# Windowed attention and routed experts in one kernel: from step 13 on, transposes of xa open the next step and the gate logits move behind the scores

## The chip, the cores and the metric

One core of a Trainium2 chip runs the whole program. The metric is the device time of one execution in microseconds (us). The program is compiled once; its instructions stand in a fixed order on each of the five engines (PE for matrix products and transposes, DVE and ACT for vector and scalar work, POOL, and SP, which issues most transfers), and engines wait for one another by semaphores. DMA engines move data between the device's memory and the on-chip buffers.

## The reference

Attention over a causal window of 64 positions, 8 batches x 8 heads x 576 positions x 64 columns, is followed by a layer of 8 experts in which each row goes to one expert. Which rows an expert gets depends on the data.

```python
def _attn_ref(q, k, v):                      # (8, 8, 576, 64)
    scores = scale * np.matmul(q, k.transpose(0, 1, 3, 2))
    mask = (rel >= 0) & (rel < 64)           # rel = row - column
    attn = softmax(np.where(mask, scores, -1e9))
    return np.matmul(attn, v)

def _moe_ref(x, modality_id, w_gate, modality_bias, w1, w2):   # x: (4608, 512)
    logits = x @ w_gate + modality_bias[modality_id]           # 8 experts
    e_idx = np.argmax(logits, axis=1)
    gate_w = softmax(logits)[rows, e_idx]
    for e in range(8):
        mask = e_idx == e
        out[mask] = gate_w[mask, None] * (np.maximum(x[mask] @ w1[e], 0) @ w2[e])
```

## The kernel before, in words

The 4,608 rows are 36 pairs of blocks (128 rows each). The outer loop is a software pipeline of steps `s` = 0 to 39; step `s` holds work on several pairs at once. From step 13 on (`s > FIRST`, `FIRST` is 12) one step runs, in the order of the code:

- `values(s-2)`: PE multiplies the softmax of pair s-2 by v into the PSUM tile `av`. `logits(s-3)`: PE multiplies `xaT` (the attention output of pair s-3, transposed) by the gate weights, DVE adds the bias (`lg`, L749). `values_out(s-2)`: DVE scales `av` into `xa` (`rw` L723, `xa` L726).
- `scores(s)`: PE, into the two PSUM tiles `sp0` and `sp1` (L659). `minima(s)`: DVE, eight masked row minima, four from each `sp` (L673). `probs_t(s-1)`: PE transposes the softmax of the pair before in two groups of four (`ss`), ACT copies each out (`pT`).
- `exps(s)`: ACT, in three portions. Between them stand four places (`gap`) that each take the next piece of expert work from the generator `slot_pieces`.
- Behind the second gap: `ranks()` in odd steps (PE counts the rows of each expert over a group of two pairs, DVE reads them into `tgt` and `cnt`), `x_t(s-2)` (PE transposes `xa` of pair s-2, ACT copies to `xaT`, L736), then `part(0)`. Behind the third gap: `part(1)`. A part prepares half the heads of q or k for a later group of two pairs: either PE transposes them ("plain" heads, tile `qk`) and DVE or ACT copies them out, or DVE transposes them itself (L585). How many heads are plain depends on the group (`n_plain`: all 8, 4 or none).

Expert work comes in slots of 256 rows, 16 pieces, so four steps. A piece `first` (L321) is 12 products of 256 columns into a quarter of the hidden layer in the PSUM tile `em`; two such pieces fill `em`, then ACT writes `hh` (L329) and DVE `hl` (L330) from it. A piece `second` (L343) is 6 products of 512 columns into `y0` or `y1`. In steps 13, 14, 15, 17, 18, 19, ... the four gaps hold first, first, second, second. In every fourth step (16, 20, ..., 36) they hold second, first, first, second, because there one slot ends and the next begins: DVE turns the next slot's rows (`xt` L283) and splits them (`xl` L196), ACT writes `xh` (L195). Until the loop ends, every `first` uses the one tile `em` (it has one buffer).

Two PSUM tiles `tp0` and `tp1` are used in turn (`turn_bank`) for what PE transposes, for the ranks and, before the change, for the logits. A tile is written again only when its last reader is done. Rows of `xa` lie in five buffers; each is scattered to memory by POOL (L828) and may be overwritten by a later `values_out` only when that transfer has landed. Work on the routing tables waits in lists (`routing`, `held`), from which `tick` and `release` put instructions on DVE.

After step 39 (from about 344 us) the program holds expert work alone.

Of the kernel before, what the change touches and what calls it, by code (L numbers as in the profile page):

```python
# [19 lines left out]
P = 128  # L20
# [6 lines left out]
def tile_window_attn_moe(  # L27
# [24 lines left out]
    GB = 2  # L52
# [476 lines left out]
    def turn_bank(s):  # L529

        i = n_tp[0]
        n_tp[0] += 1
        if s < FIRST and i % 5 > 1:
            return ps_m.tile([P, 512], F32, name=("em", "y0", "y1")[i % 5 - 2])
        return tp_bank()
# [125 lines left out]
                    rhs=kT[rows, win(c, hp), :], start=True, stop=True)  # L661
        st[p, "sp"] = sp

    def minima(p):

        sp = st.pop((p, "sp"))
        mask = masks[:, 1 if 2 * p % BPB == 0 else 2 if (2 * p + 1) % BPB == 0 else 0]
        ss = [work.tile([P, HP, P], F32, name="ss", bufs=3) for _ in range(2)]
        mn = small.tile([P, H], F32, name="mn")
        for u in range(H):  # L670
            a, hp = divmod(u, HP)
            h = 2 * hp + a
            nc.vector.tensor_tensor_reduce(  # L673
                out=ss[a][:, hp, :], in0=sp[a][:, hp * P:(hp + 1) * P], in1=mask,
                scale=-1.0 / 8.0, scalar=3.0e38, op0=ALU.add, op1=ALU.min,
                accum_out=mn[:, h:h + 1])
        sm = small.tile([P, H], F32, name="sm")
        st[p, "s"] = ss, mn, sm

    def exps(p, us):  # L680
        ss, mn, sm = st[p, "s"]
# [56 lines left out]
    def logits(p, lt):  # L738
        G, j = divmod(p, GB)
        xaT = st.pop((p, "xT"))  # L740
        for c in range(NC1):
            for i in range(2):
                cols = slice(c * P + i * W64, c * P + (i + 1) * W64)
                nc.tensor.matmul(  # L744
                    out=lt[i * W64:(i + 1) * W64, 0:E], lhsT=xaT[:, cols], rhs=wg[:, c, :],
                    start=(c == 0), stop=(c == NC1 - 1))
        if j == 0:
            st[G, "lg"] = small.tile(sh3, F32, name="lg")
        nc.vector.tensor_tensor(  # L749
            out=st[G, "lg"][:, j, :], in0=lt[:, 0:E], in1=bias_sel[:, p, :], op=ALU.add)  # L750
# [5 lines left out]
    def release():  # L756

        if held:
            tick(len(routing))
            held.pop(0)()  # L760
# [319 lines left out]
    for s in range(NPR + 4):  # L1080
        j = s % GB
        if s <= FIRST:
            for f, args in at.pop(s, ()):
                f(*args)
        n_tick = 6 if s < FIRST else 5
        n_gap = 0 if s < FIRST else 4
        G = s // GB + 1
        heads = PARTS[j] if G < NG else ()
        R = (s - 5) // GB if s >= 5 and j == 1 else -1

        def loads(n):

            for f, args in at.get(s, [])[:n]:
                f(*args)
            at[s] = at.get(s, [])[n:]

        def part(i):
            if not heads:
                return
            if 2 * 2 * i >= n_plain(G, heads[i][0]):  # L1100
                turn_heads(G, *heads[i])
                return
            tp = turn_bank(s)
            heads_t(G, *heads[i], tp)
            heads_out(tp, G, *heads[i], nc.scalar.copy if heads[i] == K1 else nc.vector.tensor_copy)

        def ranks():
            if R < 0:
                return None
            tp = turn_bank(s)  # L1110
            rk = route2(R, tp)
            n = None
            if R == NG - 1 or any(R == T for T, _ in EARLY):
                n = counts_out(tab if R == NG - 1 else pl, counts(R, tp))
            route3(R, rk)
            return n
        if 1 <= s < FIRST:
            swap_upper(s - 1)

        if 2 <= s < NPR + 2:  # L1120
            values(s - 2)
            if s <= FIRST:
                values_out(s - 2)
        if 3 <= s < NPR + 3:
            logits(s - 3, turn_bank(s) if s != FIRST else ps_m.tile([P, 512], F32, name="y0"))
            if (s - 3) % GB == GB - 1:
                route1((s - 3) // GB)
        if FIRST < s < NPR + 2:
            values_out(s - 2)
        if s < NPR:  # L1130
            scores(s)
            if s == FIRST:
                x_turn(fetched[0])
                gap(it, True)
            minima(s)
            if s == FIRST - 2:
                tick(todo[0][-1] - issued[0], table=True)
        if 1 <= s <= NPR:
            if s == FIRST:
                run_later()  # L1140
            if s >= FIRST:
                swap_upper(s - 1)
            swap_v(s - 1)
            for a in range(2):
                probs_t(s - 1, a, turn_bank(s))
            sums(s - 1)
        if s < NPR:
            exps(s, (0, 1))
        if s == 0:
            first_pair(1, (both[:1], both[1:]))  # L1150
            cast_bias()
        if s <= FIRST:
            if s >= 2:
                x_t(s - 2, turn_bank(s) if s != FIRST else ps_m.tile([P, 512], F32, name="y0"))
            run_later()
            tick(2)
            if s < NPR:
                exps(s, (2, 3, 4))
            part(0)
            if s == FIRST:  # L1160
                weights(s)
                gap(it, True)
            run_later()
            tick(n_tick)
            cnt = ranks()
            exps(s, (5, 6, 7))
        else:
            gap(it, True)
            run_later()
            release()  # L1170
            tick(2)
            if s < NPR:
                exps(s, (2, 3, 4))
            if s < FIRST + 4 or s % 2:
                weights(s)
            loads(3)
            gap(it, True)
            cnt = ranks()
            if s < NPR + 2:
                x_t(s - 2, turn_bank(s))  # L1180
            part(0)
            run_later()
            tick(n_tick)
            loads(1)
            if s < NPR:
                exps(s, (5, 6, 7))
        if n_gap > 2:
            if FIRST <= s < FIRST + 4:
                weights(s)
            gap(it, True)  # L1190
        part(1)
        run_later()
        tick(n_tick)
        if s > FIRST:
            loads(1)
        if s == WEIGHTS:
            load_weights()
        if s >= WEIGHTS:
            weights(s)
        if s > FIRST:  # L1200
            loads(9)
        if n_gap > 3:
            gap(it, True)
        run_later()
        if s == 1:
            select_bias()
        if s == 4:
            nc.sync.dma_start(out=xs_blk[DUMMY:DUMMY + 2].rearrange("b p c -> p b c"), in_=padrow)
        for T, xs_ in EARLY:
            if T == R:  # L1210
                plan(T, xs_, cnt)
# [292 lines left out]
```

## Time and profile before

| | us |
|---|---|
| median of 3 runs | 612.1 (611.96 to 615.05) |
| profiled execution | 611.99, granted clock 0.995 |
| span of its profile | 610.2 |
| PE busy in the span | 590.4 (97%) |
| DVE, ACT, POOL busy | 377.2, 283.0, 152.6 |

The profile is one execution. Its span runs from the first to the last instruction of the program; the execution's time is 1.8 us more. PE's busy time includes the modelled ends of products that overlap, so it does not say how much time could be saved; the distances between the starts of instructions do. In the rows below, "<-" in brackets names what ended the idle time before an instruction, and a tile's name stands without its buffer number.

### The profile page before, as it was taken

The page shows a single profiled execution, that of the slowest core. Times are in us where ns is not written, and L with a number is a line of the kernel's source. Part 1 is how long each engine was busy: PE and PEld are TensorE (multiplying, and loading weights), DVE is VectorE, ACT ScalarE, POOL GpSimd, SP SyncE. Part 2 cuts the span into 40 slices and gives each one's busy share as a digit, 9 for nine tenths or more (in the row PEclk, how much of TensorE's full clock was granted, in tenths as well). Part 3 has the DMA queues.
Part 4 walks back from the last instruction along what each step waited for, and adds up shares of the span by engine and source line. Part 5 has one row for each costly group of instructions (what it writes and reads, how often), then busy time and mean ns, then how long its engine had stood idle before and what let it go on. Part 6 is the DMA issues. An engine that isn't in the chain of part 4 may idle for free.

```text
span 610.2 us, 17296 instructions
## 1 busy us (share of the span) xinstructions
PE 590.4 (97%) x6257; PEld 524.7 (86%) x6257; DVE 377.2 (62%) x1479; ACT 283.0 (46%) x907; POOL 152.6 (25%) x337
## 2 busy tenths in 40 slices
PE   7998889999999999999999999999999999999996
PEld 4887778889898888988888899999999999999983
DVE  4898988877777877678755465323224634765311
ACT  3999986665657565646462111111113522653110
POOL 6323332152232331532423131011001111102102
PEclk9999999999999999999999999999999999999999
DMA  9989877685866755554513034632143544588300
GB/s 169 199 209 249 209 209 172 152 200 138 203 166 160 190 110 144 145 130 84 138 53 106 35 104 133 194 92 69 44 166 90 156 170 118 192 245 255 119 15 37
DMA packets 176615, 87.95 MB, mean 144 GB/s; under 512 B 140378, under 2 KB 158864, under 8 KB 176400
## 3 DMA queue, kind: packets, MB, share of 16 engines
q1 hardware_dynamic: 167184, 66.54, 44.8%
q0 software_dynamic: 6608, 19.71, 8.9%
q8 instruction: 50, 0.82, 0.6%
q10 hardware_dynamic: 2736, 0.58, 0.5%
q14 instruction: 37, 0.30, 0.2%
HBM read 67.36 MB, written 23.78 MB: 149 GB/s over the span
## 4 chain that ended last, share of the span: by engine, by line
PE 76%; DVE 4%; ACT 2%; issue 2%; DMA 2%; SPq 0%; POOL 0%; POOLq 0%; DVEq 0%; ACTq 0%
PE y L343 30%; PE em L321 21%; PE sp L321 10%; PE tp L483 6%; PE av L715 3%; PE sp L659 3%; PE tp L744 1%; ACT ss L685 1%; DMA qk<-in_k_dram 1%; DMA xs_scratch<-xa,idx 1%; DVE ss L673 1%; DVE xl L196 1%; DVE xt L283 1%; PE tp L393 1%; PE em L368 1%
## 5 line engine op out<-in xcount | busy, mean ns | idle before, releaser
L343 PE MATMUL y<-Whi,hh 128*128 128x512 f32 x288 | 115.8, 402 | 0.0
L685 ACT ACTIVATE ss<-ss,mn 128x128 f32<-128x128 f32 x288 | 112.2, 397 | 4.9 <-DMA y<-in_moe_modality_id_dram 2.9
L343 PE MATMUL y<-Wlo,hh 128*128 128x512 f32 x288 | 112.8, 392 | 0.0
L343 PE MATMUL y<-Whi,hl 128*128 128x512 f32 x288 | 112.4, 390 | 0.0
L354 POOL DMA_INDIRECT out_dram<-y,id x36 | 38.8, 1077 | 220.1 <-DVE y L351 156.7
L330 DVE SCALAR_TENSOR_TENSOR hl<-em,hh 128x512 fp32r<-128x512 f32 x50 | 34.5, 691 | 88.2 <-ACT hh L329 78.9
L321 PE MATMUL em<-xh,Whi 128*128 128x256 f32 x400 | 81.6, 285 | 0.3 <-issue 0.3
L321 PE MATMUL em<-xh,Wlo 128*128 128x256 f32 x400 | 79.1, 279 | 0.0
L321 PE MATMUL em<-xl,Whi 128*128 128x256 f32 x400 | 79.1, 279 | 0.0
L329 ACT ACTIVATE hh<-em 128x512 fp32r<-128x512 f32 x50 | 29.9, 598 | 105.0 <-PE em L321 88.5
L694 ACT COPY pT<-tp 128x512 f32<-128x512 f32 x57 | 31.3, 589 | 75.0 <-PE tp L483 71.4
L673 DVE CUSTOM_DVE_ANT_0 ss<-sp,masks 128x128 f32<-128x128 f32 x288 | 63.4, 285 | 2.7 <-PE sp L659 2.0
L321 PEld LDWEIGHTS em<-xh,Whi 128*128 128x128 f32 x400 | 62.8, 188 | 2.6 <-issue 0.2
L343 PEld LDWEIGHTS y<-Whi,hl 128*128 128x128 f32 x288 | 54.1, 188 | 12.1
L343 PEld LDWEIGHTS y<-Whi,hh 128*128 128x128 f32 x288 | 54.2, 188 | 9.5 <-issue 0.8
L343 PEld LDWEIGHTS y<-Wlo,hh 128*128 128x128 f32 x288 | 54.2, 188 | 8.3
L321 PEld LDWEIGHTS em<-xh,Wlo 128*128 128x128 f32 x400 | 60.9, 188 | 0.0
L321 PEld LDWEIGHTS em<-xl,Whi 128*128 128x128 f32 x400 | 60.9, 188 | 0.0
L828 POOL DMA_INDIRECT xs_scratch<-xa,idx x36 | 36.7, 1019 | 88.9 <-issue 48.9
L685 ACT ACTIVATION_READ_ACCUMULATOR ss<-ss,mn 128x1 f32 x288 | 55.9, 194 | 0.0
L329 ACT ACTIVATE hh<-sp 128x512 fp32r<-128x512 f32 x22 | 13.1, 597 | 80.5 <-PE sp L321 74.5
L715 PEld LDWEIGHTS av<-ve,pT 128*64 128x64 f32 x576 | 36.3, 138 | 12.6 <-issue 7.8
(241 smaller groups left out, 1152.9 us busy)
## 6 DMA issues: line engine op xcount, KB each, us to landing
xt<-xs_scratch SPq DMA_DIRECT2D x72, 128.0 KB
vo<-in_v_dram SPq DMA_DIRECT2D x32, 256.0 KB
y<-in_moe_w_dram SPq DMA_DIRECT2D x32, 256.0 KB
vo<-in_moe_w_dram SPq DMA_DIRECT2D x18, 256.0 KB
ss<-in_moe_w_dram SPq DMA_DIRECT2D x18, 256.0 KB
xs_scratch<-xs_scratch SPq DMA_DIRECT2D x8, 514.0 KB
pT<-in_moe_w_dram SPq DMA_DIRECT2D x12, 256.0 KB
qk<-in_k_dram SPq DMA_DIRECT2D x76, 32.0 KB
```

Source lines behind the costliest of these rows:

```text
L321: nc.tensor.matmul(out=hb[:, i * TP:(i + 1) * TP], lhsT=w[buf][:, c0:c0 + P], rhs=x[:, c * TP:(c + 1) * TP], start=(n == 0), stop=(n == le ...
L329: nc.scalar.activation(out=hh, in_=hb, func=AF.Relu),
L330: nc.vector.scalar_tensor_tensor(out=hl, in0=hb, scalar=0.0, in1=hh.bitcast(F32), op0=ALU.max, op1=ALU.subtract)))
L343: nc.tensor.matmul(out=sl["y", t], lhsT=h[:, i * TP + t * P:i * TP + (t + 1) * P], rhs=w[buf][:, c0:c0 + DM], start=(k == 0 and n == 0), s ...
L354: ins = nc.gpsimd.indirect_dma_start(out=out, out_offset=bass.IndirectOffsetOnAxis(ap=sl["id"][:, t:t + 1], axis=0), in_=y, in_offset=None ...
L483: nc.tensor.transpose(out=out_, in_=in_, identity=ident[p0:p0 + n, p0:p0 + n])
L659: nc.tensor.matmul(out=sp[a][c * W64:(c + 1) * W64, hp * P:(hp + 1) * P], lhsT=qT[rows, place(g + c, hp), :], rhs=kT[rows, win(c, hp), :], ...
L673: nc.vector.tensor_tensor_reduce(out=ss[a][:, hp, :], in0=sp[a][:, hp * P:(hp + 1) * P], in1=mask, scale=-1.0 / 8.0, scalar=3.0e38, op0=AL ...
L685: nc.scalar.activation(out=ss[a][:, hp, :], in_=ss[a][:, hp, :], func=AF.Exp, bias=mn[:, h:h + 1], scale=-1.0, accum_out=sm[:, h:h + 1])
L694: nc.scalar.copy(out=pT, in_=pp)
L715: nc.tensor.matmul(out=by_block(av)[c * W64:(c + 1) * W64, a, :, hp, :], lhsT=pT[:, i:i + W64], rhs=(vo if c else ve)[p][:, 2 * hp + a, :] ...
L828: ins = nc.gpsimd.indirect_dma_start(out=xs, out_offset=bass.IndirectOffsetOnAxis(ap=idx[:, j:j + 1], axis=0), in_=xg[j], in_offset=None)
```

## The change

Nothing is added to the computation or taken from it; from step 13 on, work changes places.

- `x_t` of pair s-3 opens step s (from step 14), where it stood as `x_t(s-2)` behind the second gap. `xaT` is thus made and used in the same step.
- `ranks()` follows `values` directly, ahead of `values_out`.
- `logits(s-3)` stands behind `scores(s)` and writes the tile `em` in place of a `tp` tile. Its DVE reader `lg` stands between the fourth and the fifth of the eight minima.
- Parts that PE transposes are both done behind the second gap; parts that DVE transposes keep their places. Both parts are plain in steps 13, 20, 21, 24, 25, 28 and 29.
- `release` is called only if something was held before this step's `ranks()`.

```diff
-    def minima(p):
+    def minima(p, us):
...
-        for u in range(H):
+        for u in us:
...
+        def part_if(i, by_pe):
+            if heads and by_pe == (4 * i < n_plain(G, heads[i][0])):
+                part(i)
...
+        def gates():
+            if 3 <= s < NPR + 3:
+                logits(s - 3, turn_bank(s) if s < FIRST else ps_m.tile([P, 512], F32, name="em" if s > FIRST else "y0"))
+                if (s - 3) % GB == GB - 1:
+                    route1((s - 3) // GB)
+        if FIRST + 1 < s < NPR + 3:
+            x_t(s - 3, turn_bank(s))
         if 2 <= s < NPR + 2:
             values(s - 2)
             if s <= FIRST:
                 values_out(s - 2)
-        if 3 <= s < NPR + 3:
-            logits(s - 3, turn_bank(s) if s != FIRST else ps_m.tile([P, 512], F32, name="y0"))
-            if (s - 3) % GB == GB - 1:
-                route1((s - 3) // GB)
+        if s <= FIRST:
+            gates()
+        else:
+            ripe = len(held)
+            cnt = ranks()
         if FIRST < s < NPR + 2:
             values_out(s - 2)
...
-            minima(s)
+            minima(s, range(H if s <= FIRST else HP))
+        if s > FIRST:
+            gates()
+        if s < NPR:
+            if s > FIRST:
+                minima(s, range(HP, H))
...
-            release()
+            if ripe:
+                release()
...
-            cnt = ranks()
-            if s < NPR + 2:
-                x_t(s - 2, turn_bank(s))
-            part(0)
+            part_if(0, False)
+            part_if(0, True)
+            part_if(1, True)
...
-        part(1)
+        if s > FIRST:
+            part_if(1, False)
+        else:
+            part(1)
```

On PE in step 18 of the program before, the end of `values` (`av`), the logits into a `tp` tile, and the first `scores`:

```order
L715 MATMUL av<-ve,pT 64x2x32
L715 MATMUL av<-vo,pT 64x2x32
L744 MATMUL tp_2955<-wg,xaT 64x8 x8
L659 MATMUL sp_2973<-kT,qT 64x128
L659 MATMUL sp_2974<-kT,qT 64x128
```

On PE in the same step of the changed program, the end of the scores, the logits, the two groups of softmax transposes (`ss`), and the first piece of expert work:

```order
L659 MATMUL sp_2958<-kT,qT 64x128
L659 MATMUL sp_2959<-kT,qT 64x128
L744 MATMUL em<-wg,xaT 64x8 x8
L483 MATMUL tp_3006<-ident_r,ss 128x128 x4
L483 MATMUL tp_3013<-ident_r,ss 128x128 x4
L321 MATMUL em<-xh,Whi_65 128x256 x2
```

The logits have moved behind the scores, and they and the expert piece write the same tile `em`, with eight transposes between them.

On DVE in step 18 of the program before, the bias addition `lg`, the scaling of `av`, and the first of the minima (each is two instructions, into `ss` and `mn`):

```order
L749 TENSOR_TENSOR lg<-tp_2955,bias_sel 128x8
L723 RECIPROCAL rw<-rs 128x16
L726 TENSOR_TENSOR xa_102<-av,rw 128x512
L673 ISA ss,mn<-sp_2973,masks 128x128
L673 ISA mn 128x1
```

On DVE in the same step of the changed program, from the last minimum of `sp0` to the first of `sp1`:

```order
L675 ISA ss,mn<-sp_2958,masks 128x128
L675 ISA mn 128x1
L749 TENSOR_TENSOR lg<-em,bias_sel 128x8
L675 ISA ss,mn<-sp_2959,masks 128x128
L675 ISA mn 128x1
```

`lg` has moved from the head of the step's DVE work to a place behind `rw`, `xa` and four minima.

On PE at the start of step 38, the last one with logits and one without values, scores or softmax transposes, in the program before:

```order
L343 MATMUL y_6559<-Wlo_67,hh 128x512
L343 MATMUL y_6559<-Whi_2520,hl 128x512
L744 MATMUL tp_6566<-wg,xaT 64x8 x8
L321 MATMUL em<-xh,Whi_2520 128x256 x2
L321 MATMUL em<-xh,Wlo_67 128x256 x2
```

The same place in the changed program:

```order
L343 MATMUL y_6552<-Wlo_67,hh 128x512
L343 MATMUL y_6552<-Whi_2513,hl 128x512
L483 MATMUL tp_6559<-ident_r,xa_101 128x128 x4
L744 MATMUL em<-wg,xaT 64x8 x8
L321 MATMUL em<-xh,Whi_2513 128x256 x2
L321 MATMUL em<-xh,Wlo_67 128x256 x2
```

The transposes of `xa`, which stood behind the second gap of step 37, now stand directly ahead of the logits that need them, and those directly ahead of the expert piece that uses the same tile.

## Rows read from the trace of the kernel before

**Rows 1.** The page, busy time of each engine, its share and instructions.

```profile
PE 590.4 (97%) x6257; PEld 524.7 (86%) x6257; DVE 377.2 (62%) x1479; ACT 283.0 (46%) x907; POOL 152.6 (25%) x337
```

**Rows 2.** Stretch, length, busy PE, PEld, DVE, ACT, POOL; clock, DMA share, GB/s.

```profile
84.01:343.63 259.62, 256.97 (x3317) 229.15 (x3317) 191.93 (x858) 149.56 (x527) 83.17 (x163) 1.00 0.57 141
343.63:610.20 266.57, 260.53 (x1689) 233.29 (x1687) 115.47 (x243) 64.76 (x117) 35.39 (x75) 0.99 0.41 126
```

**Rows 3.** PE's waits from 84 to 344 us: in all, times, longest.

```profile
PE tp L483 <- DVE lg L749: 1.6, 4, 0.5
PE tp L483 <- ACT xaT L736: 0.4, 2, 0.2
```

**Rows 4.** Timeline of PE, step 18 (start, length, line, tiles, count).

```profile
136.86 0.27 PE L715 MATMUL av<-ve,pT 128*64 128x64 f32 x1
...
137.85 0.59 PE L744 MATMUL tp<-wg,xaT 128*64 128x8 f32 x16
138.37 1.10 PE L659 MATMUL sp<-kT,qT 64*64 64x128 f32 x32
139.40 1.09 PE L483 MATMUL tp<-ident_r,ss 128*128 128x128 f32 x8
140.25 0.48 PE L321 MATMUL em<-xh,Whi 128*128 128x256 f32 x2
...
143.13 0.60 PE L483 MATMUL tp<-ident_r,xa 128*128 128x128 f32 x4
143.48 0.47 PE L343 MATMUL y<-Whi,hh 128*128 128x512 f32 x1
```

**Rows 5.** Timeline of PE, middle of step 29.

```profile
256.75 0.64 PE L483 MATMUL tp<-ident_r,xa 128*128 128x128 f32 x4
257.37 0.65 PE L483 MATMUL tp<-ident_r,qk 128*128 128x128 f32 x4
```

**Rows 6.** Timeline of DVE, step 18: the first and the fifth minimum.

```profile
139.52 0.29 DVE L673 CUSTOM_DVE_ANT_0 ss<-sp,masks 128x128 f32<-128x128 f32 x1
...
140.37 0.28 DVE L673 CUSTOM_DVE_ANT_0 ss<-sp,masks 128x128 f32<-128x128 f32 x1
```

**Rows 7.** Timeline of DVE, step 13.

```profile
86.86 0.69 DVE L330 SCALAR_TENSOR_TENSOR hl<-em,hh 128x512 fp32r<-128x512 f32 x1 [0.82 <-ACT hh L329]
87.47 0.15 DVE L749 TENSOR_TENSOR lg<-tp,bias_sel 128x8 f32<-128x8 f32 x1
```

**Rows 8.** Timelines of DVE and PE, start of step 21.

```profile
168.01 0.69 DVE L330 SCALAR_TENSOR_TENSOR hl<-em,hh 128x512 fp32r<-128x512 f32 x1 [2.54 <-ACT hh L329]
...
169.88 0.15 DVE L749 TENSOR_TENSOR lg<-tp,bias_sel 128x8 f32<-128x8 f32 x1
...
170.84 0.28 DVE L673 CUSTOM_DVE_ANT_0 ss<-sp,masks 128x128 f32<-128x128 f32 x1
...
171.24 0.36 PE L321 MATMUL em<-xh,Whi 128*128 128x256 f32 x1
```

**Rows 9.** Timelines of DVE and PE, step 33.

```profile
295.19 0.69 DVE L726 TENSOR_TENSOR xa<-av,rw 128x512 f32<-128x512 f32 x1 [2.24 <-DMA xs_scratch<-xa,idx]
...
294.40 0.48 PE L321 MATMUL em<-xh,Whi 128*128 128x256 f32 x2
```

**Rows 10.** Timelines of ACT, PE and DVE, steps 36 to 38.

```profile
319.94 0.27 PE L715 MATMUL av<-ve,pT 128*64 128x64 f32 x1
...
320.43 1.14 ACT L195 CAST xh<-xt 128x512 fp32r<-128x512 f32 x2 [0.82 <-DVE xt L283]
...
334.05 0.64 PE L483 MATMUL tp<-ident_r,xa 128*128 128x128 f32 x4
...
334.78 0.59 ACT L736 COPY xaT<-tp 128x512 f32<-128x512 f32 x1 [6.34 <-PE tp L483]
...
337.38 0.64 PE L744 MATMUL tp<-wg,xaT 128*64 128x8 f32 x16
...
338.07 0.17 DVE L749 TENSOR_TENSOR lg<-tp,bias_sel 128x8 f32<-128x8 f32 x1 [0.94 <-PE tp L744]
```

More of the change, by code (lines that the diff above doesn't have):

```diff
@@ L662, in scores @@
         st[p, "sp"] = sp
-    def minima(p):
-        sp = st.pop((p, "sp"))
+    def minima(p, us):
+        sp = st[p, "sp"]
         mask = masks[:, 1 if 2 * p % BPB == 0 else 2 if (2 * p + 1) % BPB == 0 else 0]
-        ss = [work.tile([P, HP, P], F32, name="ss", bufs=3) for _ in range(2)]
-        mn = small.tile([P, H], F32, name="mn")
-        for u in range(H):
+        if us[0] == 0:
+            st[p, "s"] = ([work.tile([P, HP, P], F32, name="ss", bufs=3) for _ in range(2)],
+                          small.tile([P, H], F32, name="mn"), small.tile([P, H], F32, name="sm"))
+        ss, mn, _ = st[p, "s"]
+        for u in us:
             a, hp = divmod(u, HP)
@@ L676, in minima @@
                 accum_out=mn[:, h:h + 1])
-        sm = small.tile([P, H], F32, name="sm")
-        st[p, "s"] = ss, mn, sm
     def exps(p, us):
```

## The prediction

> **What bounds the kernel now.** The page's busy times come first: PE 97% of the span, DVE 62%, ACT 46% [rows 1]. The table by stretch then splits the span. Steps 13 to 38, which the change touches, take 259.6 us; the expert work behind them takes 266.6 us with PE at a granted clock of 0.99 [rows 2] and holds no instruction that moves, so what PE loses or gains in the first stretch reaches the end of the program undiminished. In that stretch the waits of PE that the profile names are small: 1.6 us in four waits of softmax transposes for `lg`, 0.4 us in two waits for `xaT` [rows 3]. PE is therefore the bound, and the other engines matter only where PE must wait for them. The timeline of an undisturbed step gives PE's own lengths, from start to start: `values` 0.99 (136.86 to 137.85), logits 0.52, scores 1.03, eight softmax transposes 0.85, two `first` pieces 2.88, `x_t` 0.35 [rows 4].
>
> **Waits that go.** Softmax transposes wait for `lg` because `lg` read the `tp` tile that the second group of transposes needs. With the logits in `em` that reason is gone. The idle time is 1.6 us; from start to start the four places are each about 0.15 us longer than that, since an end is modelled 0.2 us or so behind the next possible start, which makes 2.2 us (an estimate). The plain part behind the third gap waited for ACT's copy of `xaT`, 0.4 us idle in two places and by the same correction 0.7 us; with both plain parts side by side, their `tp` tiles were last read by the `pT` copies, microseconds before. One of each pair of effects is bounded by the idle time alone: 2.0 us in all is the low end, 3.1 us the value I take (it includes about 0.2 us for shorter delays that the wait view does not list).
>
> **PE's own work.** No instruction goes, but neighbours change. `x_t` cost 0.35 us in the middle of step 18 [rows 4] and 0.62 us in step 29, where a plain part followed it [rows 5]. At the front of a step, between `second` and `values`, no row shows it; four transposes at the pitch of the softmax group (0.85 for eight) are 0.43, and 0.35 is the lowest row. Where no part follows, `first` now meets `second` directly; where two plain parts stood apart, `second` is cut once less. Bounds per step: nothing gained (0.35 against 0.35) and 0.27 us gained (0.62 against 0.35). I take 0.15 us for 24 steps, 3.6 us; the ends are 0 and 6.5.
>
> **Waits that come.** `em` has one buffer. In each step a `first` piece now waits until DVE has done `lg`, and `lg` stands behind `rw`, `xa` and four minima. Undisturbed, PE comes to that piece 0.40 + 0.99 + 1.03 + 0.52 + 0.85 = 3.8 us after the step's start (odd steps a little more, for the ranks). DVE starts its minima 0.12 us after the scores are issued (139.40 to 139.52), needs 0.85 for four (139.52 to 140.37) [rows 6] and 0.17 for `lg` [rows 10]: 0.40 + 0.99 + 1.03 + 0.12 + 0.85 + 0.17 = 3.56. So the edit is hidden by 0.2 us of softmax transposes, no more. If DVE is late by more than that, PE waits for the rest. Behind DVE's own waits everything else on DVE queues, `lg` with it. The cases:
>
> - *Step 13.* It starts at 84.01 [rows 2]. `hl` ends at 87.55 because ACT's `hh` was late [rows 7]. `hl` reads `em`, so the logits themselves cannot start before that; then `lg` follows `rw`, `xa` and four minima. From the start of an old `lg` to the first minimum are 0.96 us (169.88 to 170.84) [rows 8], so the new `lg` ends at 87.47 + 0.96 + 0.85 + 0.17 = 89.45. PE by itself would come to `first` at 84.01 + 0.99 + 1.03 + 0.52 + 0.85 = 87.4 (this step has no `x_t` in front). Wait 2.0; the 0.5 that softmax transposes waited here is in the sum above.
> - *Steps 17, 21, 25* follow a slot's end. In step 21 `hl` starts at 168.01, released by ACT, and by the same chain the new `lg` ends at 169.88 + 0.96 + 0.85 + 0.17 = 171.86 [rows 8]. ACT reaches `hh` about 0.55 us sooner, as its `xaT` copy (0.59 [rows 10], less overlap) no longer stands ahead of it: 171.3. PE came to `first` at 171.24 [rows 8]; two waits of step 20 go, about 0.8, and the step's own `x_t`, 0.4, comes in front: 170.8. Wait 0.5; I take it for the three steps, 1.5. If ACT brings nothing it is 1.1 each and as much in step 29, 4.4; if DVE starts such a step early, 0. I am nearer the low end, as the copy does leave ACT's queue by the order.
> - *Step 33.* `xa` waits until 295.19 for the landing of the scatter that empties its buffer; PE had started `first` at 294.40, untouched by it [rows 9]. Now `lg` comes 0.69 + 0.85 + 0.17 behind the start of `xa`: 296.9. Wait 2.5. The Trainium skill (PSUM — Partial Sum Buffer, section "Engine vs sequencer instructions") says that the queues of VectorE and ScalarE are strictly first in, first out. By that rule the wait of `xa` is paid by `lg` in full, as in the sum; could `lg` pass `xa`, this item would be 0 and the sum 2.5 us less. Two more steps have a shorter wait of this kind in front of `xa`; I add 0.3.
> - *Step 36.* Without scores. It starts at 319.94; ACT's `xh` runs until 321.57 [rows 10], so the copy of `xaT` ends near 322.15, and the logits wait from 319.94 + 0.40 + 0.99 = 321.3: 0.8. *Step 37.* No scores either, and `lg` stands behind the ranks' reader, `rw` and `xa`, some 0.17 + 0.24 + 0.69, and takes 0.17, while PE has only the logits, 0.52, to do: 0.75, with the signals between engines 0.9 (an estimate). *Step 38.* `x_t`, ACT's copy and the logits follow one another with nothing between. The copy starts 0.73 us after `x_t` (334.05 to 334.78) and takes 0.59; `lg` starts 0.69 after the logits (337.38 to 338.07) and takes 0.17 [rows 10]: with the signals `first` starts 2.3 us into the step, where PE alone needs 0.40 + 0.52. 1.4.
>
> New waits: 2.0 + 1.5 + 2.5 + 0.3 + 0.8 + 0.9 + 1.4 = 9.4 us.
>
> **Edits costed at nothing.** `ranks` ahead of `values_out`: PE reaches them right behind `values`, and DVE reads them in time in which it stood waiting for the logits. No transfer changes its place on SP or POOL; the scatters are released at the same step and gap as before, since what `ranks` holds back is released one step later in both versions. `xaT` in the same step has 1.03 us of scores and 0.99 of `values` as cover for 0.73 + 0.59, save in steps 36 and 38.
>
> **Sum.** 9.4 - 3.1 - 3.6 = +2.7 us on the profiled execution's 612.0, which is 0.1 below the median: 614.7 us, 0.4% slower.
>
> **The rivals.**
>
> 1. *Forecast* (0.50): waits at `em` cost a little more than the freed waits and the shorter PE work give back; 611.5 to 617.
> 2. *DVE falls behind at every slot boundary* (0.30, slower by over 0.5%). The place is the same chain hh, hl, `lg` in steps 17, 21, 25, 29. It decides if the `first` of step 21 starts more than 0.6 us behind its transposes. With 4.4 in place of 1.5: 617.6. For it: the 2.54 us that DVE stood waiting for ACT in step 21 [rows 8]; against it: the copy that leaves ACT.
> 3. *PE's shorter work and the freed waits win* (0.15, faster). If the scatter of step 33 lands before DVE needs it, and DVE is on time in 17 to 31, only 13 and 36 to 38 are left, 5.1 us; against 3.1 + 5.0 (a gain of 0.2 a step, between the middle and the upper row) the time is 609.0, and with the upper 0.27 a step 607.5. For it: PE waited for DVE four times only in this stretch [rows 3]. Against it: `lg` had no minima ahead of it then.
> 4. *The change moves only cover* (0.05): `em`'s waits appear, but the pieces behind them run closer and the sum is within 0.5 us of before, 612.
>
> **From cases to numbers.** 0.5% of 612.1 is 3.1 us, about what a measurement of this kernel tells from no change. Faster than 609.0: case 3, 0.15. Slower than 615.2: case 2 and the upper part of case 1, 0.30 + 0.10 = 0.40. The rest 0.45. The range from 609.0 to 618.5 leaves out about 0.1 on either side: its low end is case 3, its high end case 2 and 0.9 us for step 33 landing still later. The forecast alone would span 611.5 to 617.
>
> **What would show it.** Right: no wait of softmax transposes for `lg` and none of plain parts for `xaT`; instead waits of PE at L321 `em` for `lg`, largest in steps 13, 33 and 37; a wait of the logits for `xaT` in steps 36 and 38; steps 14, 18 and 22 shorter by about 0.1 us. Wrong would be: PE's waits for `lg` at `em` under 4 us in all (then 3), or over 10 (then 2); `xa` no longer waiting for its scatter in step 33; steps that lengthen without a wait, which would mean that `x_t` at the front costs more than in the middle.

## The result, and the profile after

620.1 us (median of 4, 618.3 to 620.4) against 612.0 for the kernel before on the same chip: ratio 1.0120, 95% interval 1.0085 to 1.0154. A second measurement of the same kernel (below) gave 1.0091, 1.0066 to 1.0115. Slower by about 1%, in the direction of the forecast; the first value lies above its range (609.0 to 618.5), the second in it. Kernels below are compared with the kernel before as it ran beside them on their chip; two kernels that did not run side by side are compared by these ratios and their intervals.

The page of the profiled execution (620.35 us), its busy times, beside [rows 1]:

```profile
span 618.6 us, 17305 instructions
PE 596.9 (96%) x6257; PEld 531.2 (86%) x6257; DVE 375.0 (61%) x1479; ACT 283.1 (46%) x907; POOL 154.5 (25%) x337
```

The same work takes 8.4 us longer. The table by stretch says where. Its columns are start and end, length, busy time and count of PE, PEld, DVE, ACT and POOL, PE's granted clock, DMA share, GB/s; the first seven stretches are steps 13, 14, 18, 37 and 38, the expert work, and steps 13 to 38 together, the last two the pair of `first` pieces of step 13 and of step 37.

```profile
82.72:96.82 14.10, 12.66 (x141) 11.35 (x141) 9.92 (x41) 9.04 (x30) 1.37 (x4) 0.88 0.56 133
96.82:106.95 10.13, 10.13 (x133) 9.17 (x132) 7.92 (x39) 6.93 (x24) 2.96 (x4) 1.00 0.72 177
138.82:148.53 9.71, 9.71 (x129) 8.75 (x128) 7.42 (x40) 5.98 (x22) 2.53 (x4) 1.00 0.68 150
333.03:344.15 11.12, 9.34 (x88) 8.56 (x88) 2.70 (x12) 1.18 (x2) 2.03 (x4) 0.85 0.18 67
344.15:352.05 7.90, 6.90 (x58) 5.89 (x56) 1.98 (x9) 1.40 (x3) 2.60 (x6) 1.00 0.17 65
352.05:618.60 266.55, 260.56 (x1689) 233.30 (x1688) 115.50 (x243) 64.75 (x117) 35.46 (x75) 1.00 0.41 126
82.72:352.05 269.33, 264.15 (x3318) 236.91 (x3317) 189.19 (x859) 150.16 (x526) 84.71 (x162) 0.99 0.56 137
88.19:92.66 4.47, 4.46 (x24) 4.47 (x25) 2.07 (x12) 2.88 (x12) 0.60 (x1) 0.62 0.65 123
336.92:341.38 4.46, 4.46 (x24) 4.46 (x25) 0.10 (x2) 0.00 (x0) 0.00 (x0) 0.62 0.00 0
```

Three things are to be read. The expert work takes what it took [rows 2], so the whole difference lies ahead of it: steps 13 to 38 take 269.33 in place of 259.62, 9.7 us more (step 13 happened to start 1.3 us earlier in this execution). Step 18, without any idle time, takes 9.71 us; before, from 136.86 to the start of step 19 at 146.40, it took 9.54 [rows 4], whose timeline goes on to

```profile
146.40 0.27 PE L715 MATMUL av<-ve,pT 128*64 128x64 f32 x1
```

And in steps 13 and 37 PE ran at a lower clock: their `first` pieces, 2.88 us in [rows 4], took 4.47 and 4.46 at a mean granted clock of 0.62, that is for a while at the lower of its two levels, 1.2 in place of 2.4 GHz. Against the 2.91 of step 18 in this execution that is 3.1 us in the two steps. One microsecond out of each fall (same columns):

```profile
89.00:90.00 1.00, 1.00 (x7) 1.00 (x7) 0.98 (x4) 1.00 (x7) 0.05 (x1) 0.50 0.77 146
339.00:340.00 1.00, 1.00 (x6) 1.00 (x6) 0.00 (x0) 0.00 (x0) 0.00 (x0) 0.50 0.00 0
```

PE's waits in steps 13 to 38 (us in total, times, longest), which answer to [rows 3]:

```profile
PE em L321 <- DVE lg L749: 3.1, 5, 1.8
PE em L744 <- DVE hl L330: 1.2, 1, 1.2
PE em L744 <- ACT xaT L736: 0.7, 1, 0.7
```

Softmax transposes and plain parts wait no more; `em` waits for `lg`. The second row is step 13, the third step 38. PE's timeline of step 18 (start, length, operation) shows what lengthens without a wait:

```profile
138.29 0.60 PE L483 MATMUL tp<-ident_r,xa 128*128 128x128 f32 x4
138.82 0.27 PE L715 MATMUL av<-ve,pT 128*64 128x64 f32 x1
...
139.90 0.45 PE L659 MATMUL sp<-kT,qT 64*64 64x128 f32 x8
...
140.94 0.64 PE L744 MATMUL em<-wg,xaT 128*64 128x8 f32 x16
141.51 1.09 PE L483 MATMUL tp<-ident_r,ss 128*128 128x128 f32 x8
142.36 0.48 PE L321 MATMUL em<-xh,Whi 128*128 128x256 f32 x2
...
145.27 0.39 PE L343 MATMUL y<-Whi,hh 128*128 128x512 f32 x1
...
148.01 0.60 PE L483 MATMUL tp<-ident_r,xa 128*128 128x128 f32 x4
148.53 0.27 PE L715 MATMUL av<-ve,pT 128*64 128x64 f32 x1
```

From start to start, beside [rows 4]: `x_t` 0.53 (0.35 in the middle), `values` 1.08 (0.99), scores 1.04 (1.03), logits 0.57 (0.52), softmax transposes 0.85 (0.85), `first` 2.91 (2.88), `second` 2.74 (2.92). What `x_t` costs more at the front, the two `second` pieces, now followed by `x_t` and no longer by `values`, cost less: 0.18 each. What is left is 0.17. About 0.15 of it stands where the logits were taken out (`values`, now followed by scores, 0.10 longer) and where they were put in (logits 0.05 longer), the rest in `first`.

In step 37 DVE's timeline (in brackets the idle time before and what ended it) shows why `lg` was late:

```profile
335.73 0.17 DVE L809 TENSOR_TENSOR tgt<-tp,ebase 128x16 f32<-128x16 f32 x1 [2.28 <-PE em L744]
335.82 0.24 DVE L723 RECIPROCAL rw<-rs 128x16 f32<-128x16 f32 x1
336.10 0.69 DVE L726 TENSOR_TENSOR xa<-av,rw 128x512 f32<-128x512 f32 x1
336.71 0.15 DVE L749 TENSOR_TENSOR lg<-em,bias_sel 128x8 f32<-128x8 f32 x1
```

PE's `first` starts at 336.92. `lg` stands at the end of a chain that starts with the reader of the ranks.

### The profile page after: what moved, and what is told of

Read it like the earlier page. It is cut to its first block, busy times and chain, and to the rows that moved or that the text cites. A ratio compares the mean times of both kernels' runs of the same rounds, so it can differ in the third digit from the quotient of the medians.

```text
span 618.6 us, 17305 instructions
## 1 busy us (share of the span) xinstructions
PE 596.9 (96%) x6257; PEld 531.2 (86%) x6257; DVE 375.0 (61%) x1479; ACT 283.1 (46%) x907; POOL 154.5 (25%) x337
## 4 chain that ended last, share of the span: by engine, by line
PE 63%; DVE 2%; issue 1%; POOL 0%; ACT 0%; POOLq 0%; DVEq 0%; ACTq 0%
PE y L343 27%; PE em L321 17%; PE sp L321 10%; PE tp L483 3%; PE av L715 2%; PE sp L659 2%; PE em L744 1%; PE tp L393 1%; PE em L368 1%; DVE ss L675 0%; DVE xa L726 0%; DVE y L351 0%; PE tp L848 0%; DVE rw L723 0%; PE tp L795 0%
## 5 line engine op out<-in xcount | busy, mean ns | idle before, releaser
L343 PE MATMUL y<-Whi,hh 128*128 128x512 f32 x288 | 114.5, 398 | 0.0
L321 PE MATMUL em<-xh,Whi 128*128 128x256 f32 x400 | 83.0, 289 | 3.2 <-DVE lg L749 3.1
L321 PE MATMUL em<-xl,Whi 128*128 128x256 f32 x400 | 80.4, 283 | 0.0
L675 DVE CUSTOM_DVE_ANT_0 ss<-sp,masks 128x128 f32<-128x128 f32 x288 | 65.2, 285 | 5.5 <-PE sp L659 3.4
L321 PEld LDWEIGHTS em<-xh,Wlo 128*128 128x128 f32 x400 | 62.2, 192 | 0.0
L330 DVE SCALAR_TENSOR_TENSOR hl<-sp,hh 128x512 fp32r<-128x512 f32 x22 | 15.2, 692 | 50.9 <-ACT hh L329 50.9
```

The lines of the kernel that those rows point to most:

```text
L321: nc.tensor.matmul(out=hb[:, i * TP:(i + 1) * TP], lhsT=w[buf][:, c0:c0 + P], rhs=x[:, c * TP:(c + 1) * TP], start=(n == 0), stop=(n == le ...
L330: nc.vector.scalar_tensor_tensor(out=hl, in0=hb, scalar=0.0, in1=hh.bitcast(F32), op0=ALU.max, op1=ALU.subtract)))
L343: nc.tensor.matmul(out=sl["y", t], lhsT=h[:, i * TP + t * P:i * TP + (t + 1) * P], rhs=w[buf][:, c0:c0 + DM], start=(k == 0 and n == 0), s ...
L675: nc.vector.tensor_tensor_reduce(out=ss[a][:, hp, :], in0=sp[a][:, hp * P:(hp + 1) * P], in1=mask, scale=-1.0 / 8.0, scalar=3.0e38, op0=AL ...
```

## The experiments

Most kernels were made with four sets of steps that switch the parts of the change singly. In the change they are 14 to 38, 13 to 38, and 13 to 39 twice; with all four empty the order is that of before.

```diff
-        if FIRST + 1 < s < NPR + 3:
+        if s in XT_FIRST:
             x_t(s - 3, turn_bank(s))
...
-        if s <= FIRST:
+        if s not in LG_LAST:          # logits ahead of scores, in a tp bank
             gates()
-        else:
-            ripe = len(held)
+        ripe = len(held)
+        if s in EARLY_RANKS:
             cnt = ranks()
...
-        if s > FIRST:
+        if s in LG_LAST:              # behind scores, in em
             gates()
...
+            if s not in EARLY_RANKS:
+                cnt = ranks()
+            if s < NPR + 2 and s + 1 not in XT_FIRST:
+                x_t(s - 2, turn_bank(s))
-            part_if(0, False)
+            if s in PLAIN_TOGETHER:   # else part(0) here, part(1) behind the third gap
+                part_if(0, False)
```

### One part alone, one part undone

**Old order at the edges.** `XT_FIRST` 15 to 35, `LG_LAST` and `EARLY_RANKS` 14 to 35.

> Steps 14 to 35 keep the new order; step 13 and the steps without scores (36 to 38) take the old one. Theory A (two stalls of PE, in steps 13 and 37, and the fall of the granted clock to 0.50 right behind each, are most of the loss): steps 13, 37 and 38 were 2.70, 2.87 and 1.65 us longer than before and 36 was 0.45 shorter, so 620.1 - 6.8 = 613.3 us, and no slice of the stretch at a granted clock of 0.5. Theory B (the loss lies in every step, in PE's order of small groups, and the dips of the clock come whatever the order): 617 or more, with the dips still there.

The plain heads are paired as in the change.

614.2 us, 1.0065 of before (1.0040 to 1.0090). Against the first measurement of the change about half of the loss lies in steps 13 and 36 to 38, against the second (1.0091, 1.0066 to 1.0115, on the same chip) about a third, and those two intervals overlap, so the share stays open. The rest is in the steps between. No slice of its stretch was at half clock. Both theories are half right.

**Logits alone.** `LG_LAST` 13 to 38, the others empty.

> The kernel before with only the logits moved behind scores into em. Theory A (this is the part that loses): 0.15 us of PE in each of 25 steps (3.7), waits at em in 13, 17, 21, 25, 29, 37 and the two falls of the clock (3.0): 1.012 to 1.016 of before, granted clock 0.50 behind the waits of steps 13 and 37, little different from the whole change. Rival (the loss needs the transposes at the front, which make the logits wait for xaT): under 1.006.

622.2 us, 1.0182 (1.0155 to 1.0208): this part by itself loses more than the whole change. PE stopped for 1.4 us in step 13 and 1.5 in step 37, yet the clock did not fall there. In step 33 the wait of the forecast came: `xa` waited for its scatter, and PE for `lg` behind it, 2.1 us at `em`, the longest of its waits. There, too, the clock held. Step 33 by stretch, then PE's waits for `lg` in steps 13 to 38 and that of `xa`:

```profile
297.13:309.50 12.37, 10.23 (x133) 8.90 (x132) 6.67 (x33) 5.54 (x21) 6.20 (x12) 1.00 0.62 159
...
PE em L321 <- DVE lg L749: 4.7, 6, 2.1
...
DVE xa L726 <- DMA xs_scratch<-xa,idx: 2.6, 1, 2.6
```

**Transposes of xa alone.** `XT_FIRST` 14 to 38, the others empty.

> The kernel before with only the transposes of xa moved to the front of the next step. Theory A: PE's own time stays (0.18 us more ahead of values, 0.18 less between first and second: 0.03 a step), two waits of plain parts for xaT go (0.7), three of logits for xaT come (1.9): 1.000 to 1.003 of before. By the prediction's term (0.15 us saved in 24 steps) it would be 0.995.

611.4 us, 0.9990 (0.9975 to 1.0004): no difference. The two kernels' step 22, by stretch, first `x_t` alone, then logits alone, beside that of before and of the change:

```profile
177.55:187.12 9.57, 9.57 (x130) 8.67 (x129) 7.24 (x39) 5.96 (x22) 2.25 (x3) 1.00 0.61 137
```

```profile
182.14:191.84 9.70, 9.70 (x129) 8.66 (x128) 6.55 (x36) 5.75 (x22) 2.51 (x4) 1.00 0.57 138
```

```profile
178.55:188.14 9.59, 9.59 (x129) 8.61 (x128) 6.54 (x36) 5.82 (x22) 2.27 (x3) 1.00 0.63 144
```

```profile
180.71:190.42 9.71, 9.71 (x129) 8.75 (x128) 7.19 (x38) 5.99 (x22) 2.51 (x4) 1.00 0.59 133
```

In this step, with the same work on PE and no idle time, the front place of `x_t` costs nothing and the logits' place costs all of the 0.12 (0.17 in step 18). The same holds in steps 14, 26, 30 and 34. It does not in steps 18, 20, 28 and 32 with `x_t` alone: there ACT copied `xaT` so late that the logits started late, by a delay too short for the table of waits. In step 18 (its stretch, the copy, which ends at 137.48, and the logits):

```profile
136.45:146.17 9.72, 9.72 (x129) 8.72 (x129) 7.72 (x40) 5.95 (x22) 2.27 (x3) 1.00 0.68 148
...
136.89 0.59 ACT L736 COPY xaT<-tp 128x512 f32<-128x512 f32 x1 [1.64 <-PE tp L483]
...
137.53 0.64 PE L744 MATMUL tp<-wg,xaT 128*64 128x8 f32 x16
```

`values` took 1.08 and the logits 0.57 from start to start, the lengths of the change, though logits still stood ahead of scores. So the 0.15 is lost wherever logits do not run straight on behind `values`, by order or by a late copy.

**Logits put back.** `LG_LAST` empty, the others as in the change.

> The changed kernel with logits ahead of scores again, in a bank of tp; transposes of xa still open the step. Theory A (the loss is logits behind scores: their waits at em, the clock that falls behind two of them, and 0.15 us of PE a step): the em waits go (about 5.5 us from start to start), both dips of the clock (3.0), 0.15 in 25 steps (3.7); waits of softmax transposes for lg come back (2.2): 620.1 - 10 = 610, step 18 at 9.56. Rival (the transposes at the front are what costs, 0.18 us a step and a wait for xaT in every step): 615 or more, logits waiting for xaT in most steps.

611.0 us, 1.0011 (0.9997 to 1.0025). The loss is gone; the gain hoped for beyond that did not come, since the logits waited for `xaT` in three steps (1.9 us).

**Transposes of xa put back.** `XT_FIRST` empty, the others as in the change.

> The changed kernel with the transposes of xa back in the middle of the step before; logits stay behind scores in em. Theory A (in an undisturbed step the longer PE time is that of the logits' new neighbours: values to scores +0.10, logits to softmax transposes +0.05; x_t costs 0.18 more at the front and the piece behind the place it left 0.18 less): step 18 is 9.68 us against 9.71 in the changed kernel and 9.54 before; the two waits for xaT in 36 to 38 go (0.7), em waits behind slot ends grow by some 0.35 to 0.6 each as PE comes earlier: 619 to 622. Theory of the prediction (x_t at the front saves 0.15 us in 24 steps): step 18 at 9.86 and 623.7 or more.

622.8 us, 1.0198 (1.0183 to 1.0213), steps 18 and 22 at 9.72. PE's own time is near the first theory's 9.68 and not the prediction's 9.86, and the kernel is a little slower than either end of the expected 619 to 622; the waits, however, were others than either theory had: those of the next kernel.

**Plain heads together alone.** `PLAIN_TOGETHER` 13 to 39, the others empty.

> The kernel before with only the plain heads together in the middle. Steps with two plain parts had 0.40 + 1.47 + 0.35 + 1.57 = 3.79 us for them and the last two pieces and have 0.79 + 2.85 = 3.64 in the changed kernel: 0.15 in about 12 steps, and the waits for xaT (0.7) go: 612.0 - 2.5 = 609.5. Rival: the two parts come as early as the x_t transposes and wait for a tp tile, or pT copies come later: no gain, 612.

615.6 us, 1.0079 (1.0066 to 1.0092), slower. The rival holds, and more than it said. PE's waits in its steps 13 to 38, beside [rows 3]:

```profile
PE tp L483 <- ACT xaT L736: 4.8, 6, 1.6
PE tp L483 <- DVE lg L749: 1.6, 4, 0.5
```

With `x_t` in the middle, three `tp` tiles in a row are written, and the third needs the one that ACT still has to copy to `xaT`. Side by side the parts are cheap only because `x_t` has left.

**Logits and x_t, without early ranks and pairing.** `XT_FIRST` 14 to 38, `LG_LAST` 13 to 38.

> The kernel before with logits behind scores in em and the transposes of xa at the front, without the early ranks and without the pairing of plain heads. Theory A (0.15 us of PE a step from the logits' place, em waits in 13, at slot boundaries and in 33 and 37 as in the kernel with only the logits moved; the front place of x_t takes no time of its own): 1.014 to 1.019 of before. Rival (early ranks, which put their reader on DVE ahead of lg, are what makes the waits): under 1.008.

617.6 us, 1.0126 (1.0102 to 1.0149), a little below the expected band, far above the rival's: the loss does not need early ranks.

### The clock

**Idle places filled.** The change, with transposes of the identity into a `tp` bank that nobody reads.

```diff
+        def fill(n):
+            tp = turn_bank(s)
+            n_tps[0] ^= 1
+            for i in range(n):
+                turn(tp[:, i % 4 * P:(i % 4 + 1) * P], ident)
         def gates():
+            if s == FIRST + 1:
+                fill(10)
...
+            if s == NPR + 1:
+                fill(16)
```

> The changed kernel with idle places of PE filled: 10 extra transposes of the identity ahead of the logits in step 13 and 16 behind the logits in step 37, into a tp bank that nobody reads. The waits stay as long as they are (about 1.2 and 1.8 us, now covered by work nobody needs). Theory A (the granted clock fell to 0.50 because PE stood still there): no slice at 0.50, the first piece of each of the two steps takes 2.9 us in place of 4.47, so 3.1 us less: 617.0. Rival (the clock falls at these places for another reason, such as the load of the other engines): the slices at 0.50 stay and the time stays at 620.

619.3 us, 1.0120 (1.0098 to 1.0143). Its steps 13 and 37:

```profile
84.50:97.12 12.62, 12.34 (x152) 10.87 (x151) 9.88 (x39) 9.12 (x31) 1.26 (x4) 1.00 0.63 149
333.36:343.01 9.65, 9.55 (x104) 8.72 (x104) 2.70 (x12) 1.19 (x2) 2.04 (x4) 1.00 0.21 77
```

12.62 in place of 14.10 and 9.65 in place of 11.12, at full clock, with the same instructions to wait for: in the trace 1.5 us each. Yet the median fell by 0.8 us alone and the ratio did not move. So both were run once more, side by side.

> The changed kernel as it is, beside the filled one on one chip. Theory A (the two stops of PE and the clock's fall behind them come in every execution): 1.012 of before, the granted clock at 0.50 in steps 13 and 37 again. Rival (the fall of the clock is a chance of the one profiled execution, since the kernel with only the logits moved stopped for 1.35 and 1.49 us at the same places and kept its clock): no slice at 0.50 this time, and step 13 at 12.6 us in place of 14.1.

> The filled kernel again, for its ratio to the changed kernel on the same chip. If the clock falls in every execution of the changed kernel, the filled one is 3 us (0.5%) faster; if it falls in few, the two are within 1 us.

The change: 616.8 us, 1.0091 (1.0066 to 1.0115), its executions from 614.1 to 617.9. Filled: 617.1 us, 1.0095 (1.0076 to 1.0114). The rival holds. This is the second profiled execution of the change (616.44 us): step 13, step 37, steps 13 to 38, and PE's waits in these.

```profile
84.98:97.53 12.55, 11.11 (x142) 9.80 (x141) 9.91 (x41) 9.05 (x30) 1.36 (x4) 1.00 0.65 149
332.03:340.56 8.53, 7.88 (x92) 7.15 (x91) 2.70 (x12) 1.18 (x2) 2.04 (x4) 1.00 0.23 88
84.98:348.18 263.20, 259.53 (x3318) 233.18 (x3318) 189.02 (x859) 150.45 (x526) 84.45 (x162) 1.00 0.57 140
...
PE em L321 <- DVE lg L749: 1.7, 4, 0.7
PE em L744 <- DVE hl L330: 1.2, 1, 1.2
PE em L744 <- ACT xaT L736: 0.7, 1, 0.7
```

No fall of the clock, and 263.2 against 259.6 before: 3.6 us more. The first profiled execution had 6.1 us above that: 3.1 of clock, some 1.3 of the late reader in step 37, and 1.7 in steps 17, 21, 25 and 29. The filled kernel's second execution shows a third kind of accident. In its step 33 `xa` waited for its scatter, `lg` behind it, PE for `lg`, and here the clock fell (first PE's wait, then DVE's, then the whole step and three microseconds of it):

```profile
PE em L321 <- DVE lg L749: 2.1, 1, 2.1
...
DVE xa L726 <- DMA xs_scratch<-xa,idx: 2.7, 1, 2.7
...
293.07:306.83 13.76, 11.69 (x133) 10.44 (x132) 7.09 (x33) 5.45 (x20) 6.28 (x12) 0.88 0.54 138
300.00:303.00 3.00, 3.00 (x17) 3.00 (x16) 1.20 (x4) 0.45 (x3) 0.00 (x0) 0.52 0.45 90
```

The step takes 13.76 us, against 9.98 in the first execution of the change.

### DVE's order ahead of lg

**lg ahead of the minima.** PE's order is the change's; on DVE the eight minima follow `lg`.

```diff
-            minima(s, range(H if s <= FIRST else HP))
-        if s > FIRST:
-            gates()
+            if s > FIRST:
+                gates()
+            minima(s, range(H if s <= FIRST else HP))
+        elif s > FIRST:
+            gates()
```

> The changed kernel with all eight minima behind lg on DVE; xa still ahead of lg, PE's order untouched. If lg's place behind four minima makes the waits at slot boundaries and in 13, these shrink by up to 0.85 us each and the time falls by 1 to 3 us against the changed kernel (1.004 to 1.008 of before, the changed kernel measured 1.009 to 1.012); waits behind xa (step 33) stay. Rival (the waits come from what is ahead of xa, or minima that start 0.6 us later hold up PE or ACT elsewhere): 1.009 or more.

614.8 us, 1.0055 (1.0040 to 1.0071).

**lg ahead of xa too.** As above, and `values_out(s - 2)` moved from ahead of `scores(s)` to behind `gates()`.

> As the run with lg ahead of the minima, and xa (with rw) behind lg too, so that a wait of xa for its scatter can no longer hold lg and the piece behind it. If DVE's order alone carries such waits to PE: no wait at em in step 33 above 0.3 us even where xa waits for its scatter, executions that differ by less (the changed kernel ran from 614.1 to 617.9 on one chip), and about PE's own 0.15 us a step left, with the late steps 36 to 38: 1.004 to 1.007. Rival (minima 1.6 us later each step make scores or exps late): 1.009 or more.

613.3 us, 1.0033 (1.0020 to 1.0047). PE's waits in its steps 32 to 38:

```profile
PE em L744 <- ACT xaT L736: 0.7, 1, 0.7
PE em L321 <- DVE lg L749: 0.5, 2, 0.3
```

The further `lg` stands ahead in DVE's queue, the less is lost: 1.009 to 1.012, 1.0055, 1.0033. The intervals of neighbours overlap; the change (from 1.0066 up) and the last kernel (up to 1.0047) are apart. The waits at `em` for `lg` in the profiled executions say the same, most plainly for the second move: 3.1 and 1.7 us in the change, 1.5 with `lg` ahead of the minima, 0.5 with it ahead of `xa` too. So DVE's order carries these waits. The row of the kernel with `lg` ahead of the minima:

```profile
PE em L321 <- DVE lg L749: 1.5, 4, 0.7
```

In step 33 the first of the two kernels still paid (10.54 us, `xa` waiting 1.8 for its scatter), the second did not (9.90); there `xa` comes so late that its scatter had landed, so that one could not see whether a waiting `xa` would still be harmless. The full spread did not shrink as expected (612.2 to 616.1), though nine of the ten executions lie below 613.9.

### A version from what was learnt

**Mixed.** `XT_FIRST` 14 to 37, `LG_LAST` 16, 20, 24, 28, 32, the others as in the change.

> Transposes of xa open the step up to step 37 (step 38 has them in the middle of 37, as before), ranks early, plain heads together; logits ahead of scores in a tp bank, but behind scores in em in steps 16, 20, 24, 28 and 32 alone, where the first gap is a second piece and em is free until 5.0 us into the step. Theory A: the three waits of logits for xaT seen in the run with logits first (1.9 us, steps 16, 24, 38) go, and steps 16, 20, 24, 28, 32 cost 10.17, 10.61, 10.61, 10.62, 9.73 as in the changed kernel: 1.4 + 0.8 less than that run: 0.997 of before, 608.8. Rival (what a step gains is lost again at the next slot boundary, where DVE is then late): 1.000 of before.

610.5 us, 0.9975 (0.9962 to 0.9988), against 611.8 for before on that chip. It beats both kernels, the one before by 0.25%; a wait of 1.0 us for `xaT` in step 24 stayed.

**Mixed, x_t early where logits come last.** As mixed, without 16, 20, 24, 28, 32 and 36 in `XT_FIRST`.

> The mixed kernel (logits ahead of scores, but behind them in em in steps 16, 20, 24, 28, 32), with the transposes of xa in the middle of the step before for just these steps and 36, and at the front elsewhere. Theory A (in these steps the logits wait for xaT, which ACT copies only behind xh; 1.0 us in step 24 of the mixed kernel): that wait goes, steps 16 to 32 by fours lose the 0.5 at their front, steps 15 to 31 gain 0.35 in their middle: 0.996 of before. Rival (the copy of xaT moves into the middle of 15, 19, 23, 27, 31 and holds up a part's tp there): 1.000.

610.1 us, 0.9987 (0.9975 to 0.9999). The wait went, but the ratio is no better than the mixed kernel's; the intervals overlap, and the two ran on different chips.

## Why the prediction was right and wrong

**What bounds.** Right: the expert work kept its length to 0.02 us, and all that PE lost in steps 13 to 38 reached the end.

**Waits that go (-3.1).** Right in kind: neither of the two rows of [rows 3] is left. For the plain parts it holds only because `x_t` moves as well.

**PE's own work (-3.6).** This is the step that failed. It priced the new neighbours of `x_t` and of the parts, taking 0.15 us gained in 24 steps, but not those of the logits. Measured: `x_t` at the front 0 where `xaT` is in time (9.57 against 9.59 with `x_t` alone), the logits behind scores 0.11 to 0.18 lost in each of the undisturbed steps 14, 18, 22, 26, 30 and 34 (9.70 and 9.72 in steps 22 and 18 with the logits alone, 9.59 and 9.54 before). Over 24 steps that is 3 to 4 us on the other side, some 7 us from the forecast, more than the whole distance from 614.7 to 620.1. The lost time has no row in the table of waits; it shows only between starts. Why PE starts scores 0.1 us later behind `values` than it starts logits there, no run shows. The rows hold one pattern that no run tests by itself. The field ahead of the shapes in PE's rows is 128*64 for `values` and logits, 64*64 for scores and 128*128 for all else. In step 18 or 22 it changes three times before and with `x_t` alone, four times in the change and with logits alone, and `values` is the longer only where it changes right behind them or the logits come late.

**Waits that come (+9.4).** The mechanism was right: `em` couples PE to a DVE queue in which `lg` has a chain ahead of it, and with that chain taken from ahead of `lg` most of the loss goes. The sum was too high: the listed waits come to 5.0 us in the first execution and 3.6 in the second. Items were sized from one execution of the kernel before:
- Step 13: 2.0 forecast. 1.2 at the logits, for `hl`, and 0.3 at `em` in both executions.
- Slot boundaries: 0.5 forecast in each of three steps, 1.5. Listed were 0.6 in step 17 and 0.2 in step 21 in the first execution and 0.5 in step 25 in the second. Delays too short for that table come on top: step 29, without a listed wait in either, took 11.49 us in the first and 10.79 in the second.
- Step 33: 2.5 forecast. Nothing in both profiled executions of the change, where `xa` waited only 0.3 and 0.4 us; but PE waited 2.1 us in the filled kernel's second and 2.1 with the logits alone, 1.4 with logits and `x_t`, and 0.3 to 0.8 in three others. The mechanism is there and its size was about right; how much of it strikes changes with the landing of the scatter. In the change's first execution PE came to that step 4.1 us later than before (294.68 against 290.62), which may be why the scatter had nearly landed; with the logits alone it came later still (297.13) and waited. The Trainium skill (PSUM — Partial Sum Buffer, section "Engine vs sequencer instructions") has VectorE's queue strictly in order; the trace agrees: where `xa` waited for 2.7 us, `lg` did wait behind it.
- Step 36: 0.8 forecast, none came. Step 37: 0.9 forecast; 1.8, and 1.29 us from logits to `first` in the second execution (333.27 to 334.57 in its trace) where logits alone need 0.57. Step 38: 1.4 forecast, 0.7 for `xaT` and 0.3 for `lg`.

**Left out.** That a stop of PE can cost as much again by the clock. In the first execution two stops brought 3.1 us, as much as all of PE's waits for `lg`.

**The sum.** The forecast had waits at +6.3 (9.4 less 3.1) and PE's own work at -3.6. In the second execution steps 13 to 38 took 3.6 us more: listed waits +1.6 (3.6 against the 2.0 of [rows 3]), and the other 2.0 in no wait's row. In the first they took 9.7 more: waits +3.0, the clock 3.1, and 3.6 in no row. So half of the loss, without the clock, came by a term that the forecast had with the wrong sign, and that the second measurement lies in the range is luck: an error of some 6 us in PE's own work met one of some 5 us in the waits.

**The tests named.** "Waits under 4 us in all, then faster" was wrong: they were 3.1 and the kernel was slower, since the waits were not the only term. "Steps that lengthen without a wait" came true (steps 14, 18 and 22 are 0.1 to 0.2 us longer, not 0.1 shorter), but its reading (`x_t` costs more at the front) did not; it was the logits.

## What to carry to other kernels

Where one engine is the bound, price a moved group of small products by both its old and its new neighbours, from start to start, and compare an undisturbed step: a tenth of a microsecond that no wait shows, 24 times, weighed about as much as all the waits here. A shared tile that ties the bounding engine to the end of another engine's queue can turn an accident on that queue (a late scatter, a late reader) into a stop; put the reader first in the queue or keep the tile apart. Parts of a change may hold only together: pairing the plain heads lost 0.8% by itself, and with the transposes gone from their place its waits are gone too.

## What the runs showed of the hardware

The granted clock fell to 0.50 behind some stops of PE and not behind others as long or longer. It fell behind 1.2 and 0.3 us (step 13) and behind 1.8 us (step 37) in the first execution of the change, and behind 2.1 us in the filled kernel. It did not fall behind the same 1.2 and 0.3 us in the change's second execution, nor behind 1.4, 1.5 and 2.1 us with the logits alone. The plainest case lies ahead of step 13, in a part that the change does not touch: in every one of the 16 profiled executions PE stops there for 1.85 us (2.00 in one), and the clock fell behind it in one alone, that of the second mixed kernel (the wait, and the stretch behind it):

```profile
79.93 0.66 PE L483 MATMUL tp<-ident_r,Whi 128*128 128x128 f32 x4 [1.85 <-ACT pT L694]
...
81.00:84.40 3.40, 3.40 (x18) 3.40 (x17) 3.20 (x11) 3.40 (x17) 0.00 (x0) 0.50 0.03 10
```

The Trainium skill (TensorE: Matmul & The Clock Gate, section "HAM oscillation — how this bites in real kernels") tells of an engine that idles between groups of products and runs the next at half clock. The trace agrees where it happened, 2.9 us of pieces taking 4.5; the stops that were enough here are shorter than the waits it tells of. What decides between the two cases stays open, as does why DVE's reader of the ranks began 1.6 us behind them in step 37 (334.12 to 335.73), and why one measurement of the change gave 1.012 and the other 1.009.
